# Windowed attention and a squared-ReLU network: where the weights' combinations are made, and how deep their stream runs

## The chip, the cores and the metric

One core of a Trainium2 chip runs the whole program. The metric is the device time of one execution in microseconds (us); a smaller number is better. The engines are named as in the profile: PE (TensorE matmuls), PEld (the loading of PE's stationary operand), DVE (VectorE), ACT (ScalarE), POOL (GpSimd) and SP (SyncE, whose queue issues every DMA of this kernel).

## The reference, cut to what matters

```
# q, k, v: 8 batches x 8 heads x 576 tokens x 64, float32
scores = (q @ k.T) / sqrt(64)
mask   = (0 <= i - j) & (i - j < 64)            # a window of 64 tokens
attn   = softmax(where(mask, scores, -1e9))
x      = (attn @ v), heads side by side         # 4608 tokens x 512
h = x @ w_in                                    # 512 x 2048
r = maximum(h, 0)
out = (r * r) @ w_out                           # 2048 x 512
```

## The kernel before, in words

**Precision.** The large products keep float32 accuracy by splitting each operand into a high part and a rest (`hi`, `lo`, both fp32r), so that each product is three matmuls: hi by hi, hi by lo, lo by hi.

**Tiles and sections.** The 4608 tokens are 12 tiles of 384. The attention is cut into 36 sections, three to a tile. A section's operations have one letter each in `section`: S (scores on PE), o and s (the part of the window that is wanted, copied on ACT and DVE), z and y (negated maximum), e and f (two halves of the exponentials on ACT), k and R (sums and reciprocals), m (the multiplication by the reciprocal, on POOL), X (transposes on PE), x (masked copy on DVE), V (attention by values on PE), H and Q (high part and rest of the result, into the tile that the network reads). Q is only needed for the first four tiles.

**The network.** Tiles 0 to 3 (`NPLAIN = 4`) are done plainly: 16 blocks `f` of the hidden width for each, and for each block 12 matmuls of the first stage (`mm1`, letter M, line 398), then r, p, g, G (ReLU, square, high part and rest: lines 407, 412, 415, 417), then 9 matmuls of the second stage (`mm2`, letter O, line 440), two blocks behind (`LAG = 2`). Tiles 4 to 11 are done in four pairs: the first stage of a pair is a two by two block product with seven products in place of eight (`product`, line 879, 6 matmuls each), in 8 steps for each pair, and the second stage (`second`, line 963) follows two steps behind, three calls of 12 matmuls a step.

**The weights' combinations.** Four of the seven products take a combination of blocks of the first-stage weights rather than a block itself. These are made once, in 16 pieces `h`, by `mix`, and written to a DRAM tensor `mixed`: A (six POOL instructions, lines 526 and 528), C (high part, on ACT, line 530), E (rest, on POOL, line 532), F (the DMA, line 534). A piece works in one half, `h % 2`, of a wide SBUF tile. That tile takes the place of `a_t`, in which the weights are split, so the first A waits for the end of that splitting (operation l15, line 131). The split weights themselves are written to DRAM (`kept`) as well.

**What sets the order.** Up to the second block of tile 2 the order on every engine is written by hand: the string `order`, one token per operation, and each engine does its own operations in the order of the string. From there on `Plan` makes the order: each operation is given an engine, a cost, what it reads and writes, and how long after it its data has landed; `in_order` gives each engine, whenever it comes free in the model, the ready operation with the earliest due time, where due times are counted back from PE's fixed sequence. The order that comes out is fixed before the program runs; on the chip each engine, SP's queue too, works strictly in it.

**What the change touches.** Pieces 0 to 9 (`NMIX = 10`) are in the string, between M22 and M33, together with the sections 6 to 9; pieces 10 to 15 are in the plan, beside tiles 2 and 3. Tiles 4 and 5 are held in the wide tile, tile 4 in half 0 and tile 5 in half 1, so their sections come after the pieces that use the same half. In tiles 2 and 3 a burst of one section (`burst`) is put into PE's sequence at the blocks that `starts` lists: S of section i, V of section i - 1; X of section i comes two blocks later (`crosses`).

In the paired part every product fetches its weight block (256 KB, `wi_fetch`, line 706) into one of 8 slots (`NWI`), each again free when its product is done; every block of the second-stage weights (512 KB, `wo_fetch`, line 714) goes into one of 8 slots (`NWO`). The same SP queue issues the loads of q and k (line 145, eight DMAs a call) and of v (line 154). The seven operands of a pair's products (differences of the tiles' quarters, split into high part and rest) are made by `operands`.

Of the kernel before, what the change touches and what calls it, by code (L numbers as in the profile page):

```python
# [15 lines left out]
P = 128  # L16
# [12 lines left out]
def window_attention_relu2_ffn(ctx: ExitStack, tc: tile.TileContext, q, k, v, w_in, w_out, out):  # L29
# [188 lines left out]
    def section(op, i, eng=None):  # L218
# [81 lines left out]
        else:  # L300
            hi, lo = get_x(i // SPT)
            ps = ps_x[i].rearrange("p m (w q) -> p m w q", q=QB)
            for d, nd, w0, r0, n in regions:
                cols = slice(r0 * QB, (r0 + n) * QB)
                h, l = hi[:, :, d:d + nd, cols], lo[:, :, d:d + nd, cols]
                vals = ps[:, :, w0:w0 + nd * n].rearrange("p m (d r) q -> p m d (r q)", d=nd)
                if nd == 1:
                    h, l, vals = h[:, :, 0], l[:, :, 0], vals[:, :, 0]
                if op == "H":
                    copier(eng or "a")(h, vals)  # L310
                else:
                    dve.tensor_tensor(l, vals, h.bitcast(F32), ALU.subtract)
# [40 lines left out]
    def out_tile(t):  # L353
        if ("out", t) not in xs:
            xs["out", t] = ffn.tile([P, NTB, DM], F32, name="x0" if t else "x1")
        return xs["out", t]
# [117 lines left out]
    while n1 < NF:  # L474
# [24 lines left out]
        g26 F3 Q6 z8 X7 r27 C4 E4 G26 y8 M28 A6 p27a x7 e8 D5 O26 g27 F4 f8 G27 q7 V7 r28 C5 E5 k8 R8 p28a m8p  # L499
        S9 g28 F5 H7d M29 A7 G28 Q7 o9d v10 X8 r29 C6 E6 s9 M30 A8 p29a x8 g29 F6 z9 v11 V8 r30 C7 E7 D6 y9 f9  # L500
        M31 A9 p30d H8a e9 Q8 O27 k9 R9 m9p G29 O28 g30 F7 r31 C8 E8 p31d X9 G30 g31 F8 O29 x9 D7 G31 M32 O30
        r32 C9 E9 p32d g32 F9 M33 G32 O31 r33 Z31 W31 p33d g33 G33"""
# [14 lines left out]
    def mix(op, h):  # L517
        p, kk = divmod(h, 2)
        flat = wide()[:, h % 2].rearrange("p a b c -> p (a b c)")
        scr = flat[:, :4 * P].rearrange("p (a b) -> p a b", a=4)  # L520
        mx = flat[:, 4 * P:12 * P].bitcast(F32R).rearrange("p (a b c) -> p a b c", a=4, b=2)
        if op == "A":
            for c in range(2):
                hi, lo = (wparts[2 * p + c][:, 0, part].bitcast(F32).rearrange("p (a k c) -> p a k c", a=2, k=2)[:, :, kk]
                          for part in range(2))
                pool.tensor_tensor(scr[:, 2 * c:2 * c + 2], hi, lo, ALU.add)  # L526
            for to, a, b, how in ((3, 2, 3, ALU.add), (2, 0, 2, ALU.subtract), (0, 3, 0, ALU.subtract), (1, 1, 0, ALU.subtract)):
                pool.tensor_tensor(scr[:, to], scr[:, a], scr[:, b], how)  # L528
        elif op == "C":
            act.copy(mx[:, :, 0], scr)  # L530
        elif op == "E":
            pool.tensor_tensor(mx[:, :, 1], scr, mx[:, :, 0].bitcast(F32), ALU.subtract)  # L532
        else:
            sp.dma_start(mixed[p, :, :, :, kk * P:(kk + 1) * P], mx.bitcast(F32))
# [77 lines left out]
    def operand(n):  # L612
        if n in (0, 2, 3):
            x = slab(f"xb{max(0, n - 1)}", F32R)[:, :4 * TT].rearrange("p (a b c) -> p a b c", a=2, b=2)
        elif n > 4:
            x = x_tile(3)[:, n - 5]
        else:
            if "x" not in xs:
                xs["x"] = ffn.tile([P, 2, 2, 2, TT], F32R, name="x0")
            x = xs["x"][:, n // 4]  # L620
        return x
# [4 lines left out]
    class Plan:  # L626
# [16 lines left out]
        def in_order(self):  # L643
# [22 lines left out]
            while len(out) < len(ops):  # L666
# [24 lines left out]
    HOP, NEAR = 0.12, 0.05  # L691
# [9 lines left out]
    def wi_fetch(name, source, keys=()):  # L701
# [5 lines left out]
             freed(f"wi{slot // 4}") if n < NWI else [])  # L707

    def wo_fetch(name, f):
        n = wo_n[0]  # L710
        wo_n[0] += 1
        slot = n % NWO
        wo[name] = slot
        plan("sp", 0.1, lambda: sp.dma_start(wo_slot(slot).bitcast(F32), kept[f, :, 1]), [], [("wo", slot)], 6.0,
             freed(f"wo{slot // 2}") if n < NWO else [])
# [6 lines left out]
    def held(i):  # L722
# [3 lines left out]
        return [("XF", half, m, i % SPT) for m in range(2)] + ([("mix", half)] if i // SPT < NPLAIN + 2 else []), []  # L726
# [44 lines left out]
    def settle(i):  # L771
# [3 lines left out]
        plan("act", 0.56, by(section, "H", i), ["v_ps0", "v_ps1"], hi)  # L775
# [3 lines left out]
    def burst(i, late=None):  # L779
        scores(i)  # L780
        values(i - 1 if late is None else late)
        weigh(i)
        settle(i - 1 if late is None else late)
# [3 lines left out]
    def plain1(n):  # L787
# [4 lines left out]
        plan("pe", 1.95, do, [(x, t % 2, r) for x in ("xh", "xl") for r in range(SPT)] + [("w", f)], [("bank", 0)])  # L792
# [33 lines left out]
    def operands(j):  # L826
        keys = {(m, half): [("XF", half, m, r) for r in range(SPT)] for half in range(2) for m in range(2)}
        b = {mh: (lambda m=mh[0], half=mh[1]: wide()[:, half, m], keys[mh]) for mh in keys}
# [8 lines left out]
        def split(n, x):  # L837
            dead = []
            if first and n in (0, 2, 3):
                dead = freed(f"xb{max(0, n - 1)}")  # L840
            elif first:
                dead = [(y, 1, r) for y in ("xh", "xl") for r in range(SPT)] if n > 4 else [("x", tb) for tb in range(NTB)]
# [11 lines left out]
        sub("dve", b[1, 0], b[1, 0], t[1])  # L854
        split(5, b[1, 0])
# [9 lines left out]
    def product(s, n):  # L865
# [16 lines left out]
        plan("pe", 0.98, do, [("xo", n, 0), ("xo", n, 1), ("wi", slot)], [key])  # L882
# [45 lines left out]
    def second(k, x):  # L928
# [49 lines left out]
    starts = {2: 10, 5: 11, 8: 12, 11: 13, 14: 14, 17: 15, 20: 16, 23: 17, 26: 18}  # L978
    crosses = {n + 2: i for n, i in starts.items()}
    for h in range(NMIX, 2 * NP):  # L980
        mixing(h)
    for n in range(2 * NF + LAG, NPLAIN * NF):
        m = n - 2 * NF
        plain1(n)
        if m in starts:
            burst(starts[m])
# [4 lines left out]
        if m % 3 == 0 and 10 <= 9 + m // 3 < NF:  # L991
            plan("sp", 0.1, by(keep, 9 + m // 3), [("w", 9 + m // 3), ("r", n % 2)], [], 8.0)
# [61 lines left out]
```

## Time and profile before

| | us |
|---|---|
| median of 3 runs | 883.92 |
| the runs | 881.0, 883.92, 888.91 |
| the profiled execution | 883.67 |
| its span, first to last instruction | 882.0 |
| PE busy / PEld busy | 842.4 / 770.7 |
| DVE / ACT / POOL busy | 581.9 / 407.7 / 206.0 |
| mean granted TensorE clock | 0.981 |

A row of instructions in the profile gives the line, the engine, the operation, what is written and read, the count, then busy time, the mean in nanoseconds of one, and the idle time ahead of them with what ended it. The chain is the sequence of work that ended last, followed back from the last instruction; its rows give start, duration and what was done, with the count of instructions merged. The matmul rows of the chain are the time by which the chain moved on, a little under the busy time of the same matmuls. The table by windows gives busy time and count of each engine in a stretch, then the granted clock, the share of the DMA engines that was busy and GB/s.

### The profile page before, as it was taken

To read this page: it belongs to the slowest core of one execution; us is meant where nothing else is said; L and a number is where in the kernel's file an instruction comes from. 1 tells how busy PE (TensorE), PEld (TensorE's weight loads), DVE (VectorE), ACT (ScalarE), POOL (GpSimd) and SP (SyncE) were. 2 spreads that over 40 slices of the span, in tenths; PEclk is the share of its full clock that TensorE was granted. 3 is DMA by queue.
4 is the path that set the end of the run, shared out by engine and by line. 5 is a ranking of instruction groups with operands and counts; after the bars stand their busy time and mean duration, and the time that the engine had idled before them with its cause. 6 is when DMAs were issued, how large, how long until landed. Compare 5 with 4: busy or idle time off the path is not lost.

```text
span 882.0 us, 17771 instructions
## 1 busy us (share of the span) xinstructions
PE 842.4 (96%) x6754; PEld 770.7 (87%) x6754; DVE 581.9 (66%) x870; ACT 407.7 (46%) x1127; POOL 206.0 (23%) x258
## 2 busy tenths in 40 slices
PE   6899999779999999999799999999999999999998
PEld 5688998669999998999699998998999999999997
DVE  5799996454575567667368665678765668545553
ACT  5787874554454644554334344434345424222221
POOL 1210008685731112112131111140121141101010
PEclk9899999788999999999899999999999999999999
DMA  9989948575576467849875789968695574767521
GB/s 216 225 265 323 348 168 172 111 161 153 180 180 174 138 124 194 275 123 222 169 231 170 217 237 184 268 200 212 224 280 154 173 232 134 255 232 240 150 104 71
DMA packets 273012, 173.92 MB, mean 197 GB/s; under 512 B 190496, under 2 KB 239648, under 8 KB 270880
## 3 DMA queue, kind: packets, MB, share of 16 engines
q1 hardware_dynamic: 272928, 172.80, 69.9%
q8 instruction: 53, 0.87, 0.4%
q14 instruction: 31, 0.25, 0.1%
HBM read 138.15 MB, written 34.60 MB: 196 GB/s over the span
## 4 chain that ended last, share of the span: by engine, by line
PE 75%; POOL 6%; SPq 5%; DMA 5%; DVE 4%; issue 3%; ACT 2%; POOLq 0%; DVEq 0%; ACTq 0%
PE banks L963 27%; PE banks L879 24%; PE banks L440 9%; PE banks L398 8%; PE banks L232 3%; PE banks L295 3%; POOL a L528 2%; SPq L145 2%; POOL a L526 2%; ACT sel L260 1%; DMA w<-in_moe_w_out_dram 1%; PE banks L273 1%; SPq L182 1%; POOL a L532 1%; DVE a L122 1%
## 5 line engine op out<-in xcount | busy, mean ns | idle before, releaser
L963 PE MATMUL banks<-w 128*128 128x512 f32 x1152 | 258.3, 381 | 0.0
L963 PEld LDWEIGHTS banks<-w 128*128 128x128 f32 x1152 | 216.5, 190 | 28.7
L879 PE MATMUL banks<-x,w 128*128 128x384 f32 x768 | 137.6, 329 | 7.7 <-DMA w<-mixed 4.2
L398 PE MATMUL banks<-x,w 128*128 128x384 f32 x768 | 139.8, 333 | 3.0 <-ACT r L407 2.7
L440 PE MATMUL banks<-w,g 128*128 128x512 f32 x576 | 138.1, 386 | 0.1
L398 PEld LDWEIGHTS banks<-x,w 128*128 128x128 f32 x768 | 129.3, 193 | 7.7 <-ACT r L407 4.9
L879 PEld LDWEIGHTS banks<-x,w 128*128 128x128 f32 x768 | 127.0, 190 | 9.6 <-issue 5.6
L905 POOL TENSOR_TENSOR g<-g 128x384 f32<-128x384 f32 x64 | 57.7, 906 | 320.9 <-ACT g L916 306.8
L440 PEld LDWEIGHTS banks<-w,g 128*128 128x128 f32 x576 | 107.6, 191 | 14.7 <-DVE g L417 1.3
L879 PE MATMUL banks<-w 128*128 128x384 f32 x576 | 107.4, 332 | 0.0
L260 ACT ACTIVATE sel<-sel,nm 128x64 f32<-128x64 f32 x272 | 90.8, 335 | 29.9 <-POOL nm L254 14.9
L879 PEld LDWEIGHTS banks<-w 128*128 128x128 f32 x576 | 96.3, 191 | 2.0
L971 DVE TENSOR_TENSOR w<-w,banks 128x512 f32<-128x512 f32 x72 | 49.4, 686 | 71.2 <-PE banks L963 71.2
L269 POOL TENSOR_TENSOR sel<-sel,nm 128x512 f32<-128x512 f32 x33 | 35.9, 1089 | 145.9 <-DVE nm L266 81.1
L953 ACT CAST w<-w 128x512 fp32r<-128x512 f32 x48 | 29.8, 620 | 73.0 <-PE banks L963 73.0
L953 ACT CAST w<-g 128x512 fp32r<-128x512 f32 x48 | 29.6, 620 | 63.9 <-PE banks L963 61.9
L407 ACT ACTIVATE r<-banks 128x384 f32<-128x384 f32 x64 | 31.6, 493 | 56.8 <-PE banks L398 55.7
L417 DVE TENSOR_TENSOR g<-r,g 128x384 fp32r<-128x384 f32 x64 | 40.8, 639 | 19.5 <-ACT g L415 14.3
L893 DVE TENSOR_TENSOR w<-banks,r 128x384 f32<-128x384 f32 x64 | 38.2, 596 | 20.7 <-PE banks L879 20.5
L260 ACT ACTIVATION_READ_ACCUMULATOR sel<-sel,nm 128x1 f32 x272 | 51.0, 187 | 0.0
L412 DVE TENSOR_TENSOR r<-r 128x384 f32<-128x384 f32 x38 | 25.7, 677 | 35.7 <-ACT r L407 35.7
L277 DVE TENSOR_TENSOR pt<-banks,masks 128x1024 f32<-128x1024 f32 x33 | 40.2, 1218 | 11.7 <-PE banks L273 11.7
(89 smaller groups left out, 1005.0 us busy)
## 6 DMA issues: line engine op xcount, KB each, us to landing
w<-mixed SPq DMA_DIRECT2D x128, 256.0 KB, 4.8
w<-kept SPq DMA_DIRECT2D x64, 512.0 KB, 7.0
w<-kept SPq DMA_DIRECT2D x96, 256.0 KB, 4.9
kept<-w SPq DMA_DIRECT2D x16, 1024.0 KB, 9.0
vt<-in_v_dram SPq DMA_DIRECT2D x144, 64.0 KB, 3.9
w<-in_moe_w_in_dram SPq DMA_DIRECT2D x16, 512.0 KB, 7.4
w<-in_moe_w_out_dram SPq DMA_DIRECT2D x16, 512.0 KB, 8.3
mixed<-a SPq DMA_DIRECT2D x16, 512.0 KB, 3.7
```

The lines of the kernel that those rows point to most:

```text
L260: act.activation(sels[i][:, w, hd], sels[i][:, w, hd], AF.Exp, bias=nms[i][:, n], scale=SCALE, accum_out=sums[i][:, n])
L269: (dve if eng == "d" else pool).tensor_tensor(p, p, rs[i][:, :, None].broadcast_to([P, SW * 2, QB]), ALU.mult)
L277: dve.tensor_tensor(pts[i].rearrange("p (w n) q -> p w n q", n=2), ps_t[i][:, :, None, :].broadcast_to([P, SW, 2, P]), masks.rearrange("p ...
L398: pe.matmul(h_ps, lhsT=weights(kk, part), rhs=in_turn(x[xx][:, kk // 2, kk % 2]), start=n == 0, stop=n == 3 * NK - 1)
L417: dve.tensor_tensor(gs[n][1], rg.pop(n), gs[n][0].bitcast(F32), ALU.subtract)
L440: pe.matmul(acc(t, tb), lhsT=gg[:, ts], rhs=in_turn(weights(part)), start=f == 0 and n == 0, stop=f == NF - 1 and n == 2)
L879: pe.matmul(ps[:, :TT], lhsT=w[:, part, kk * P:(kk + 1) * P], rhs=in_turn(x[:, xx, kk]), start=n < 4 and m == 0, stop=m == 5, skip_group_c ...
L893: plan("dve", 0.6, lambda: dve.tensor_tensor(to(), ps, other(), ALU.add), [kps, ko], keys, 0, after)
L905: plan("pool", 0.95, lambda: pool.tensor_tensor(x(), x(), x(), ALU.mult), [], keys)
L953: plan("act", 0.62, lambda: act.copy(high(c), src()), g_keys, [kh], 0, freed("hi") if new else [])
L963: pe.matmul(ps, lhsT=gg[:, m // 2, m % 2], rhs=in_turn(wo_slot(w[m])[:, part]), start=m == 0 and n == 0, stop=m == 3 and n == 2)
L971: plan("dve", 0.72, lambda: dve.tensor_tensor(by_half(parts(tb)), by_half(parts(tb)), ordered(ps), ALU.add), [key], [kp])
```

## The change

1. `NMIX` goes from 10 to 4: pieces 0 to 3 stay in the hand-written order, now close together between M21 and M25 (A0 C0 E0 A1 C1 E1 and so on, with C right behind its A), and pieces 4 to 15 are in the plan. There A is planned as six single operations, and E goes to DVE instead of POOL; a piece's DMA is planned to land after 5.0 us instead of 8.0.
2. Tile 4 is no longer held in the wide tile but in the second half of the buffer `x0`, whose first half takes tile 2's output; so its sections wait for the end of tile 2's first stage instead of the pieces that use half 0.
3. The sections of tiles 4 and 5 are two deep: after the S of section i comes V of section i - 2, and at the same block, behind the second stage, X of section i - 1. `starts` and `crosses` are rewritten; section 17's V is at block 28 (it was at 26).
4. `NWI` goes from 8 to 13. The five new slots are the unused last quarters of the slabs xb0, xb1, xb2, hi and lo.
5. A fetch of second-stage weights is tied to a product (`tick`): one after each of the products 0, 2, 4 and 6 of every second step, instead of four as soon as their slots are free.
6. The seven operands are laid out otherwise; the first pair's three differences go to DVE instead of POOL.
7. The plan takes 1.5 us instead of 0.12 from an operation of another engine than PE to an SP operation that waits for it.

```diff
-NWI = 8
+NWI = 13
-NMIX = 10
+NMIX = 4
...
     def get_x(t):
...
-        return wide()[:, t % 2], wide()[:, t % 2]
+        if t == NPLAIN:
+            out_tile(2)
+            return xs["out", 2][:, 1], None
+        return wide()[:, t % 2], None
...
         order = """ ...
-        l15 p21a g21 q3 G21 M22 A0 O21 r22 p22d g22 G22 M23 A1 D2 O22 r23 C0 E0 p23d q4 g23 F0 M24 A2 G23 Z22
-        W22 O23 r24 C1 E1 p24d g24 F1 G24 S6 M25 A3 o6a D3 q5 s6 O24 r25 C2 E2 z6 p25a y6 g25 F2 f6 G25 S7 O25
-        e6 o7d s7 v9 k6 z7 M26 A4 R6 y7 m6p f7 D4 X6 e7 q6 S8 x6 r26 C3 E3 k7 V6 R7 o8a p26d m7p M27 A5 H6a s8
+        l15 A0 p21a g21 C0 E0 q3 G21 M22 A1 O21 r22 F0 p22d g22 C1 E1 G22 M23 A2 D2 O22 r23 F1 p23d q4 g23 C2 E2
+        M24 A3 G23 Z22 W22 O23 r24 F2 p24d g24 C3 E3 G24 S6 M25 o6a D3 q5 s6 O24 r25 F3 z6 p25a y6 g25 f6 G25 S7
+        O25 e6 o7d s7 v9 k6 z7 M26 R6 y7 m6p f7 D4 X6 e7 q6 S8 x6 r26 k7 V6 R7 o8a p26d m7p M27 H6a s8 g26 Q6 z8
... (the rest of the string: the same tokens with the pieces 4 to 9 taken out)
+    def wi_home(n):
+        return (f"wi{n // 4}", n % 4) if n < 8 else (("xb0", "xb1", "xb2", "hi", "lo")[n - 8], 3)
...
-                    soon[m] = max(soon[m], start + cost + lands + HOP)
+                    hop = SPARE if ops[m][0] == "sp" and engine != "pe" else HOP
+                    soon[m] = max(soon[m], start + cost + lands + hop)
...
-        plan("pool", 2.9, by(mix, "A", h), w, key)
+        for c in range(6):
+            plan("pool", 0.77 if c < 2 else 0.5, by(mix, "A", h, [c]), w if c < 2 else [], key)
         plan("act", 0.6, by(mix, "C", h), [], key)
-        plan("pool", 1.3, by(mix, "E", h), [], key)
-        plan("sp", 0.1, by(mix, "F", h), key, [("mixed", h // 2, h % 2)], 8.0)
+        plan("dve", 0.7, by(mix, "E", h, dve), [], key)
+        plan("sp", 0.1, by(mix, "F", h), key, [("mixed", h // 2, h % 2)], 5.0)
...
-        sub("pool", t[0], b[0, 1], b[0, 0])
-        sub("pool", t[1], b[1, 1], t[0])
-        sub("pool", b[0, 1], b[1, 1], b[0, 1])
+        eng = "dve" if first else "pool"
+        sub(eng, t[0], b[0, 1], b[0, 0])
+        sub(eng, t[1], b[1, 1], t[0])
+        sub(eng, b[0, 1], b[1, 1], b[0, 1])
...
-        if half == 0 and x == 0:
-            for f in range(4 * group, 4 * group + 4):
-                wo_fetch((j, f), f)
...
-    starts = {2: 10, 5: 11, 8: 12, 11: 13, 14: 14, 17: 15, 20: 16, 23: 17, 26: 18}
-    crosses = {n + 2: i for n, i in starts.items()}
+    starts = {2: (10, 9), 5: (11, 10), 9: (12, 11), 13: (13, 0), 16: (14, 12), 18: (15, 13), 21: (16, 14), 23: (17, 15),
+              26: (18, 16), 28: (0, 17)}
+    crosses = {4: 10, 7: 11, 11: 12, 16: 13, 18: 14, 21: 15, 23: 16, 26: 17, 30: 18}
...
             for n in range(7):
                 product(s, n)
+                if s % 2 == 0 and n % 2 == 0:
+                    f = s % NP * 2 + n // 2
+                    wo_fetch((s // NP, f), f, [("tick", s, n)])
```

A pair in the new `starts` is (section whose S comes here, section whose V comes here); 0 stands for none.

More of the change, by code (lines that the diff above doesn't have):

```diff
@@ L354, in out_tile @@
         if ("out", t) not in xs:
-            xs["out", t] = ffn.tile([P, NTB, DM], F32, name="x0" if t else "x1")
-        return xs["out", t]
+            xs["out", t] = ffn.tile([P, 2, 2, 2, TT], F32, name="x0" if t else "x1")
+        return xs["out", t][:, 0].rearrange("p a b c -> p (a b c)").rearrange("p (n e) -> p n e", n=NTB)
     def slab(name, dtype, words=4 * DM):
@@ L514, in keep, with mix @@
         sp.dma_start(kept[f], wparts[f].bitcast(F32))
-    def mix(op, h):
+    def mix(op, h, which=None):
         p, kk = divmod(h, 2)
@@ L522, in mix @@
         if op == "A":
[L523 to L528, printed above, removed]
+            for c in which or range(6):
+                if c < 2:
+                    hi, lo = (wparts[2 * p + c][:, 0, part].bitcast(F32).rearrange("p (a k c) -> p a k c", a=2, k=2)[:, :, kk]
+                              for part in range(2))
+                    pool.tensor_tensor(scr[:, 2 * c:2 * c + 2], hi, lo, ALU.add)
+                else:
+                    to, a, b, how = ((3, 2, 3, ALU.add), (2, 0, 2, ALU.subtract), (0, 3, 0, ALU.subtract),
+                                     (1, 1, 0, ALU.subtract))[c - 2]
+                    pool.tensor_tensor(scr[:, to], scr[:, a], scr[:, b], how)
         elif op == "C":
@@ L531, in mix @@
         elif op == "E":
-            pool.tensor_tensor(mx[:, :, 1], scr, mx[:, :, 0].bitcast(F32), ALU.subtract)
+            (which or pool).tensor_tensor(mx[:, :, 1], scr, mx[:, :, 0].bitcast(F32), ALU.subtract)
         else:
@@ L612, in operand @@
     def operand(n):
[L613 to L621, printed above, removed]
+        if n < 3:
+            return slab(f"xb{n}", F32R)[:, :4 * TT].rearrange("p (a b c) -> p a b c", a=2, b=2)
+        if n < 5:
+            return x_tile(3)[:, n - 3]
+        if "x" not in xs:
+            xs["x"] = ffn.tile([P, 2, 2, 2, TT], F32R, name="x0")
+        return xs["x"][:, n - 5]
     FULL = (NTILE - NPLAIN) // 2
@@ L689, in in_order @@
             return [ops[n][2] for n in out]
-    HOP, NEAR = 0.12, 0.05
+    HOP, NEAR, SPARE = 0.12, 0.05, 1.5
     plan = Plan()
@@ L706, in wi_fetch, with wo_fetch @@
         plan("sp", 0.1, lambda: sp.dma_start(wi_slot(slot).bitcast(F32), source), keys, [("wi", slot)], 4.5,
-             freed(f"wi{slot // 4}") if n < NWI else [])
-    def wo_fetch(name, f):
+             freed(wi_home(slot)[0]) if n < NWI else [])
+    def wo_fetch(name, f, tick):
         n = wo_n[0]
@@ L713, in wo_fetch @@
         wo[name] = slot
-        plan("sp", 0.1, lambda: sp.dma_start(wo_slot(slot).bitcast(F32), kept[f, :, 1]), [], [("wo", slot)], 6.0,
+        plan("sp", 0.1, lambda: sp.dma_start(wo_slot(slot).bitcast(F32), kept[f, :, 1]), tick, [("wo", slot)], 6.0,
              freed(f"wo{slot // 2}") if n < NWO else [])
@@ L725, in held @@
             return [("xh", i // SPT % 2, i % SPT)], [("xl", i // SPT % 2, i % SPT)]
-        return [("XF", half, m, i % SPT) for m in range(2)] + ([("mix", half)] if i // SPT < NPLAIN + 2 else []), []
+        return [("XF", half, m, i % SPT) for m in range(2)] + ([("mix", half)] if 4 < i // SPT < 7 else []), []
     def scores(i):
@@ L774, in settle, with burst @@
         hi, lo = held(i)
-        plan("act", 0.56, by(section, "H", i), ["v_ps0", "v_ps1"], hi)
+        plan("act", 0.56, by(section, "H", i), ["v_ps0", "v_ps1"], hi, 0,
+             [(x, 0, r) for x in ("xh", "xl") for r in range(SPT)] if i // SPT == NPLAIN else [])
         if lo:
             plan("dve", 0.68, by(section, "Q", i), ["v_ps0", "v_ps1"] + hi, lo)
-    def burst(i, late=None):
+    def burst(i, j):
         scores(i)
-        values(i - 1 if late is None else late)
+        values(j)
         weigh(i)
-        settle(i - 1 if late is None else late)
+        settle(j)
     def plain1(n):
@@ L791, in do @@
             hs[n] = mm1(t, f, lambda kk, part: wparts[f][:, 0, part, kk * P:(kk + 1) * P])
-        plan("pe", 1.95, do, [(x, t % 2, r) for x in ("xh", "xl") for r in range(SPT)] + [("w", f)], [("bank", 0)])
+        plan("pe", 1.95, do, [(x, t % 2, r) for x in ("xh", "xl") for r in range(SPT)] + [("w", f)],
+             [("bank", 0), ("tick", n)])
         plan("act", 0.49, by(evac, "r", n), [("bank", 0)], [("r", n % 2)])
@@ L838, in split @@
             dead = []
-            if first and n in (0, 2, 3):
-                dead = freed(f"xb{max(0, n - 1)}")
+            if first and n < 3:
+                dead = freed(f"xb{n}")
+            elif first and n < 5:
+                dead = [(y, 1, r) for y in ("xh", "xl") for r in range(SPT)]
             elif first:
-                dead = [(y, 1, r) for y in ("xh", "xl") for r in range(SPT)] if n > 4 else [("x", tb) for tb in range(NTB)]
+                dead = [("x", tb) for tb in range(NTB)] + keys[0, 0] + keys[1, 0]
             plan("act", 0.75, lambda: act.copy(operand(n)[:, 0], x[0]()), x[1], [("xo", n, 0)], 0, dead)
@@ L853, in operands @@
         split(4, b[1, 0])
-        sub("dve", b[1, 0], b[1, 0], t[1])
-        split(5, b[1, 0])
+        sub("dve", t[0], b[1, 0], t[1])
+        split(5, t[0])
         split(6, b[1, 1])
@@ L881, in do @@
                     m += 1
-        plan("pe", 0.98, do, [("xo", n, 0), ("xo", n, 1), ("wi", slot)], [key])
+        plan("pe", 0.98, do, [("xo", n, 0), ("xo", n, 1), ("wi", slot)], [key, ("tick", s, n)])
         b, a, c, d = (sums_of.get((s, m), (None, None)) for m in range(4))
@@ L985, in window_attention_relu2_ffn @@
         if m in starts:
-            burst(starts[m])
+            burst(*starts[m])
         plain2(n - LAG)
```

18 lines of the change are left out of this document (9 added, 9 removed).

## The prediction

> **What bounds the kernel now.** First I read the table by windows, for where PE is idle at all: only there can a change that removes no matmul gain time. Columns: stretch, its length, busy time of PE, PEld, DVE, ACT, POOL, granted clock, DMA share, GB/s.
>
> ```profile
> 140.00:160.00 20.00, 16.94 (x142) 14.78 (x140) 10.52 (x14) 9.77 (x30) 15.87 (x25) 0.97 0.83 190
> 160.00:180.00 20.00, 15.93 (x205) 14.36 (x205) 7.83 (x11) 11.65 (x45) 15.51 (x25) 0.77 0.47 99
> 180.00:200.00 20.00, 14.19 (x97) 12.54 (x96) 12.21 (x19) 8.08 (x27) 17.84 (x28) 0.83 0.71 157
> ...
> 220.00:240.00 20.00, 20.00 (x175) 18.62 (x174) 10.97 (x20) 9.19 (x32) 14.53 (x19) 1.00 0.61 196
> ...
> 420.00:440.00 20.00, 13.77 (x126) 12.37 (x125) 8.05 (x16) 6.13 (x24) 2.61 (x3) 0.89 0.83 173
> ```
>
> Two holes lie behind the start-up: 140 to 200, where PE is idle for 12.9 us and the clock is down to 0.77, and 420 to 440, 6.2 us. Nearly everywhere else PE is at 20 of 20. Next the chain, for what fills the first hole.
>
> ```profile
> by line: POOL a L528 23.0%; POOL a L526 17.4%; POOL a L532 13.2%; ACT sel L260 10.4%; PE banks L440 8.9%; issue 7.2%; PE banks L398 5.8%; POOL sel L269 4.4%; ACT r L407 1.6%; DVE w L131 1.5%; PE banks L273 1.4%; ACT a L530 1.3%; POOL nm L26
> ...
> 134.88 1.70 POOL a L526 x2
> ...
> 155.10 0.22 POOL nm L254
> ...
> 155.34 2.77 ACT sel L260 x16
> ...
> 197.34 1.12 PE banks L273 x4
> 198.45 3.84 PE banks L440 x9
> ...
> 204.82 1.29 PE banks L440 x6
> ```
>
> From 134.88 (A0) to 197.34 (X9) the chain runs over POOL: A and E are 54% of 128 to 206. The sections' small POOL operations (y, k, m) wait behind them, PE waits for the sections. O30 starts at 204.82; I use it as the marker. For the second hole, the chain and then SP's queue:
>
> ```profile
> 407.30 7.10 PE banks L879 x42
> ...
> 424.27 3.51 DMA w<-kept
> ...
> 451.62 7.02 PE banks L879 x42
> ```
>
> ```profile
> 406.51 3.13 SPq L714 DMA_DIRECT2D w<-kept  x4
> 409.69 10.05 SPq L154 DMA_DIRECT2D vt<-in_v_dram  x8
> 419.85 0.55 SPq L145 DMA_DIRECT2D raw<-in_q_dram  x1
> ...
> 424.27 0.45 SPq L706 DMA_DIRECT2D w<-kept  x1
> ```
>
> Products start at 407.30, 424.27 and 451.62: one step of 16.97 us, then one of 27.35. From 406.51 to 424.27 SP issues four second-stage fetches, eight loads of v and eight of q and k, and no weight block for a product; with 8 slots for 7 products a step, PE has used what was there by then.
>
> **Part 1: the hand-written order, pieces 0 to 9 become 0 to 3.** The rows with the durations, first PE's (S, V, O, X and M in the chain), then the groups:
>
> ```profile
> 326.05 0.93 PE banks L232 x32
> 326.98 0.89 PE banks L295 x40
> ...
> 336.79 1.94 PE banks L440 x9
> 338.74 0.44 PE banks L273 x4
> 339.17 1.95 PE banks L398 x12
> ```
>
> ```profile
> L528 POOL TENSOR_TENSOR a<-a 128x128 f32<-128x128 f32 x64 | 32.6, 509 | 5.0
> ...
> L526 POOL TENSOR_TENSOR a<-w 128x256 f32<-128x256 f32 x32 | 24.6, 789 | 80.1 <-DVE w L131 79.6
> ...
> L269 POOL TENSOR_TENSOR sel<-sel,nm 128x512 f32<-128x512 f32 x33 | 35.9, 1089 | 145.9 <-DVE nm L266 81.1
> ...
> L532 POOL TENSOR_TENSOR a<-a 128x512 fp32r<-128x512 f32 x16 | 21.6, 1354 | 14.7 <-ACT a L530 14.7
> ...
> L954 DVE TENSOR_TENSOR w<-w 128x512 fp32r<-128x512 f32 x48 | 33.2, 691 | 14.0 <-ACT w L953 14.0
> ...
> L530 ACT CAST a<-a 128x512 fp32r<-128x512 f32 x16 | 9.8, 616 | 2.0 <-POOL a L528 2.0
> ```
>
> With gaps between instructions A is 4.0 us (2 of 789 ns, 4 of 509), C 0.62, E 1.35. The new order puts C right behind its A and E behind that, so POOL stands still during each C: 4.0 + 0.7 + 1.4 = 6.1 us a piece. Walked from A0 at 134.88: A0 ends at 138.9, C0 139.6, E0 141.0; A1 145.0, C1 145.7; A2 151.1, C2 151.8; A3 157.2, C3 157.9, E3 159.2. y6 comes behind E3, at about 160, where it was at 155.10: this part is first **later**, not earlier. ACT is held too: r22 stands behind C0, r23 behind C1, r24 behind C2 and the output copies, o6 behind C3, and each next M needs that r's bank. An M taking 1.95 and an O 1.94, PE waits 1.2 us before M23, 2.2 before M24, 2.9 before M25 and 1.4 before S7. The section chain then runs freely: e and f 2.77 us together, k and R 0.4, m 1.09, so X6 stands at 164.8; before it was at 163.30.
>
> Behind X6 no piece is left. PE's work from X6 to O30 is four X, two S, three V, six M and four O: 1.8 + 1.9 + 2.7 + 11.7 + 7.8 = 25.9 us. I add 1.5, an estimate from the durations, for V6 and V8 behind their x (1.22) and X8 behind Q7: O30 at 192.2. Against 204.82 that gains 12.6. I take **-11**: the walk leaves nothing for engines that meet, and waits of up to 2.9 us cost clock, as these rows show (second column the time):
>
> ```profile
> 182.76 1.02 PE L273 MATMUL banks<-ident,sel 128*128 128x128 f32 x4 [2.57 <-DVE x L312]
> ...
> 183.43 3.58 PE L398 MATMUL banks<-x,w 128*128 128x384 f32 x12
> ```
>
> After 2.57 us of idleness four transposes took 1.02 and an M 3.58 in place of 1.95; before M25 that would be about 2 us, of which ACT and POOL, still behind until 160, hide most. Bounds: if only the two later waits of PE, 2.57 and 3.25 us, go and X6 is 1.5 later, -4; if PE is never kept waiting behind X6, -14. The Trainium skill, "TensorE: Matmul & The Clock Gate" (Part 1), puts the fall to half rate after an idle window of about 3.4 us; by it none of the walk's waits would slow PE and this term would be nearer the walk's -12.6. The row shows the fall after 2.57, so the row decides.
>
> **Part 2: tiles 2 and 3 take six pieces more.** Twelve pieces are 12 x 3.6 = 43 us of POOL (nine m, 10 us, come to that) in some 150 us, 7.4 us of C on ACT, 8.3 us of E on DVE at L954's 691 ns. The row 220:240 has mixing beside bursts of sections, with POOL at 14.53, and PE at 20.00; DVE (10.97) and ACT (9.19) have room. So I cost it at nothing; the cover is PE's own matmuls. The wait that takes the place of another: in the new `starts`, X of one section comes one O (1.94 us) behind V of another, in the same bank, and H must come between. These rows price it:
>
> ```profile
> L310 ACT COPY a<-banks 128x256 f32<-128x256 f32 (+3 forms) x38 | 15.0, 433 | 5.3 <-PE banks L295 4.3 <-DMA raw<-in_k_dram 0.6 <-DVE w L954 0.2
> ...
> 334.57 2.22 PE L398 MATMUL banks<-x,w 128*128 128x384 f32 x12 [0.68 <-ACT r L407]
> ```
>
> H is 0.43 us and half a group of exponentials ahead of it on ACT 1.4 (2.77 / 2), so six joints can each cost 0 to 1. The other end is below nothing: the wait of 0.68 us above, of an M for an r that stood behind exponentials, may go. I take +0.5, range -0.7 to +6.
>
> Queued DVE work is the term's risk. The Trainium skill, "SBUF — State Buffer" (the shared port pair), says that a DVE instruction with two SBUF inputs and a POOL instruction exclude each other for their whole length. It speaks against this change, which puts more POOL work beside DVE's g - hi and E. By it each such pair costs one of them the other's length, up to 0.8 us a time. In the row 220:240 the two are busy for 25.5 of 20 us together, so they do not exclude each other always; no row here shows the lock by itself.
>
> **Part 3: the hand-over to the pairs.** Section 17's V is the row at 326.98 above; the products began here, and the rows under it price the operands:
>
> ```profile
> 354.74 6.83 PE banks L879 x42
> ```
>
> ```profile
> L844 DVE TENSOR_TENSOR x<-a,x 128x768 fp32r<-128x768 f32 x16 | 15.2, 947 | 0.2 <-ACT x L843 0.2
> ...
> L834 DVE TENSOR_TENSOR a<-a,w 128x768 f32<-128x768 f32 x4 | 5.4, 1350 | 0.0
> ```
>
> 26.9 us of cover lay between; V moves two blocks of 3.9 us, so 19 us (a stall of 0.7 taken off 26.9) less 1 remain, about 18. What must fit: H 0.8, two differences of 1.35, one more, a split of 0.95 on DVE: the first operand by 7 us, all seven by about 19, where the sixth and seventh product need theirs at 18 + 5. DVE also has to do p, G and section 18's steps, some 8 us. It fits with little left: +0.5, range 0 to 5 (each of the four differences taking twice its time).
>
> **Part 4: 13 slots, second-stage fetches spread.** SP's hole of 17.8 us lies beside a step of 17.0. With 13 slots the fetches issued ahead reach 12 products ahead at the start of the hole: the next step's first six blocks are there at 424.27, and its seventh is issued first behind the hole, 6 us before its product. What is late next: nothing that PE reads, since SP catches up in the following step (7 fetches of 0.45 us, 3.2 in all). Gain 27.35 - 17.05 = 10.3, clock loss within it. A smaller stall of the same kind:
>
> ```profile
> 515.13 7.02 PE banks L879 x42
> ...
> 534.38 4.94 DMA w<-mixed
> ...
> 550.58 7.02 PE banks L879 x42
> ```
>
> Its two steps took 35.45 against 34.1: 1.3. Together **-11**, taking both as gone but 0.6; bounds 0 (SP's total of issues is the same, and the jam only moves) and -11.6. The ticks put fetches a step behind their present place, yet the second stage reads them two steps, 34 us, later: nothing.
>
> **The sum.** 883.67 (the profiled execution; median of the runs 883.92) - 11 + 0.5 + 0.5 - 11 = **862.7 us**. 1% of the time is 8.8 us, about what this measurement can tell from no change.
>
> **The rivals.**
> Both holes shrink: 862.7, own range 856 to 869. Chance 0.60.
> *The first hole only moves.* The four pieces hold ACT and POOL until 159, and the sections behind them take as long as before: part 1 gives -2, the rest holds: 871.7. For it: y6 is 5 us later by my walk. Against: 54% of that chain is A and E, and six of ten are gone. 0.14.
> *The second hole only moves.* SP's issues are the limit in the first pair and the 13 slots only put the stall into a later step: 873.7. For it: 17.8 us without a pause in SP's rows. Against: five slots more cover 5 products, and behind 451.62 the longest such stall is the one of 1.3 us. 0.12.
> *Tiles 2 and 3 lose what is gained*, by the joints and operands at their upper ends (+6 and +5) and part 4 half: 883.7 - 11 + 6 + 5 - 5.5 = 878. 0.08.
> *The pieces stall PE in tiles 2 and 3.* C waits in ACT's queue for an A that POOL, kept off by DVE, ends late; r stands behind C, and the next M behind r, as in my walk of M23 to M25: 2.1 us of wait and about 2 of slow clock for each of twelve pieces, +49; with the rest kept, 912. It decides once POOL falls behind its plan by more than a block (3.9 us). Against: no such wait from 204 to 320 with six pieces there. This is also what the rule of the port pair would make of the time. 0.06.
>
> **How the numbers follow.** Under 875: the first case, nearly all of the second, and most of the third: 0.82. Within 1%: the fourth and the rest, 0.12. Slower: 0.06. Range 856 to 876: it holds the first three cases; what is left out is the last two and a little.
>
> **What would show it.** In the changed profile: O30 some 11 us earlier than 204.82, y6 later than 155.10, POOL no more in the chain behind 165; waits of PE for ACT's r before M23 to M25; PE at 20 of 20 from 200 to 340 with E on DVE at 0.7; no wait of products for `mixed` or `kept`, and every step with a section at 17.1. I am wrong if PE waits for ACT in tiles 2 and 3, if the first product of the pairs waits for its operands, or if SP's queue is again ahead of PE with loads while slots stand empty.

## The result, and the profile after

The changed kernel took **861.70 us** (median of 4 runs, 861.0 to 863.32) beside 883.67 (881.0 to 888.91) for the kernel before on the same chip: ratio 0.9747, 95% interval 0.97 to 0.9794. The forecast was 862.7, with a range of 856 to 876. The profiled execution took 862.08, its span is 860.3 (before 883.67 and 882.0), so the spans differ by 21.7.

Two matters of reading first. The lines of the helpers have moved: M is now L401, O is L443, the products are L894, the second stage L975; A is L529 and L533, C L535, E L537. And five marks cut the span into parts that can be set beside each other: the end of l15 (the last instruction ahead of A0), X6, O30, the first product of the pairs, and the end.

The table by windows, the same stretches as before:

```profile
140.00:160.00 20.00, 15.37 (x125) 12.13 (x124) 10.72 (x13) 7.04 (x14) 16.80 (x24) 1.00 0.75 176
160.00:180.00 20.00, 16.48 (x215) 14.72 (x215) 11.70 (x20) 12.97 (x58) 8.63 (x18) 0.91 0.48 91
180.00:200.00 20.00, 19.86 (x144) 18.16 (x143) 11.95 (x18) 8.54 (x28) 1.52 (x3) 1.00 0.68 146
220.00:240.00 20.00, 20.00 (x172) 18.61 (x171) 13.31 (x24) 10.05 (x33) 10.02 (x15) 1.00 0.53 175
420.00:440.00 20.00, 20.00 (x173) 18.51 (x172) 14.59 (x23) 8.27 (x27) 8.99 (x7) 1.00 0.92 206
```

The hole at 420 is gone. Of the first one 8.2 us of idleness are left between 140 and 180 (4.63 and 3.52); from 180 to 200 PE is at 19.86 of 20, where before it had 14.19. The chain from 128 to 206, by line and then in order of time:

```profile
by line: PE banks L401 24.3%; PE banks L443 19.1%; POOL a L533 14.7%; POOL a L529 12.7%; POOL a L537 6.5%; PE banks L295 5.9%; PE banks L232 4.2%; ACT a L535 3.2%; issue 2.6%; ACT r L410 1.9%; DVE w L131 1.5%; PE banks L273 1.4%; POOL sel L
...
133.15 1.70 POOL a L529 x2
...
157.29 3.13 POOL a L529 x4
160.42 0.20 POOL nm L254
160.63 3.32 POOL a L533 x8
...
165.75 0.66 PE banks L273 x4
...
195.04 1.94 PE banks L443 x9
```

A and E are 34% of it, not 54, and behind X6 (165.75) POOL is off the chain. O30 starts at 195.04 in place of 204.82. But between E3, which ends at 157.22, and y6 (L254) stand four instructions of A that the string has nowhere near.

The chain in the pairs, where each first product of a step begins:

```profile
344.10 3.39 PE banks L894 x21
347.50 6.03 DMA w<-kept
...
353.54 8.96 DMA vt<-in_v_dram
...
363.77 7.02 PE banks L894 x42
...
380.92 7.02 PE banks L894 x42
...
397.99 7.02 PE banks L894 x42
...
414.94 7.02 PE banks L894 x42
...
431.99 7.02 PE banks L894 x42
```

17.15, 17.07, 16.95 and 17.05 us a step; the last of them, from 414.94, is the one that took 27.35 before (from 424.27). Part by part, with the experiments told of below (all in us; each column is the length of the stretch up to the mark):

| kernel | end of l15 | to X6 | to O30 | to the first product | to the end |
|---|---|---|---|---|---|
| before | 134.81 | 28.5 | 41.5 | 149.92 | 527.26 |
| after | 133.08 | 32.7 | 29.3 | 149.06 | 516.20 |
| after_8slots | 133.02 | 32.6 | 29.3 | 149.07 | 526.32 |
| before_13slots | 133.31 | 28.3 | 41.3 | 149.70 | 514.56 |
| after_one_block | 135.58 | 30.1 | 28.2 | 149.06 | 516.93 |
| old_places | 131.56 | 24.9 | 29.3 | 149.07 | 515.90 |
| after_0pieces | 133.98 | 22.0 | 28.1 | 169.66 | 516.57 |
| odd_pieces_early | 133.05 | 22.0 | 28.1 | 149.07 | 515.89 |
| odd_no_ticks | 133.42 | 22.0 | 28.1 | 149.06 | 514.63 |
| after_no_ticks | 133.34 | 32.6 | 29.6 | 149.07 | 514.82 |
| after_E_on_pool | 130.85 | 32.6 | 29.2 | 149.06 | 516.61 |

The 21.7 us of after against before are 1.7 in the start, 8.0 from l15 to O30 (70.01 to 61.96), 0.9 in tiles 2 and 3, and 11.1 in the pairs. The first of them is no gain of the change: up to l15 the hand-written order is the same in all eleven kernels, and l15 ends anywhere from 130.85 to 135.58.

### The profile page after: what moved, and what is told of

Its sections match the earlier page's. It is cut to its first block, busy times and chain, and to the rows that moved or that the text cites. A ratio compares the mean times of both kernels' runs of the same rounds, so it can differ in the third digit from the quotient of the medians.

```text
span 860.3 us, 17706 instructions
## 1 busy us (share of the span) xinstructions
PE 832.6 (97%) x6754; PEld 762.0 (89%) x6754; DVE 591.1 (69%) x885; ACT 409.0 (48%) x1127; POOL 186.4 (22%) x243
## 4 chain that ended last, share of the span: by engine, by line
PE 81%; DMA 5%; POOL 4%; SPq 3%; DVE 3%; issue 2%; ACT 1%; DVEq 0%; POOLq 0%; ACTq 0%
PE banks L975 29%; PE banks L894 25%; PE banks L443 9%; PE banks L401 9%; PE banks L295 3%; PE banks L232 3%; DMA w<-in_moe_w_out_dram 3%; PE banks L273 1%; POOL a L533 1%; SPq L182 1%; POOL a L529 1%; DMA vt<-in_v_dram 1%; DVE a L122 1%; SPq L154 1%; DMA w<-kept 1%
## 5 line engine op out<-in xcount | busy, mean ns | idle before, releaser
L975 PE MATMUL banks<-w 128*128 128x512 f32 x1152 | 257.5, 380 | 0.0
L975 PEld LDWEIGHTS banks<-w 128*128 128x128 f32 x1152 | 215.7, 189 | 28.4
L401 PE MATMUL banks<-x,w 128*128 128x384 f32 x768 | 137.6, 329 | 4.0 <-ACT r L410 3.5
L443 PE MATMUL banks<-w,g 128*128 128x512 f32 x576 | 136.6, 382 | 1.0 <-DVE g L420 0.8
L401 PEld LDWEIGHTS banks<-x,w 128*128 128x128 f32 x768 | 126.7, 189 | 9.0 <-ACT r L410 6.4
L894 PE MATMUL banks<-x,w 128*128 128x384 f32 x768 | 130.0, 326 | 0.0
L894 PEld LDWEIGHTS banks<-x,w 128*128 128x128 f32 x768 | 125.7, 189 | 0.0
L443 PEld LDWEIGHTS banks<-w,g 128*128 128x128 f32 x576 | 106.0, 189 | 16.0 <-DVE g L420 2.8
L894 PE MATMUL banks<-w 128*128 128x384 f32 x576 | 100.7, 329 | 0.0
L894 PEld LDWEIGHTS banks<-w 128*128 128x128 f32 x576 | 93.8, 189 | 2.0
L965 ACT CAST w<-g 128x512 fp32r<-128x512 f32 x48 | 29.6, 621 | 62.1 <-PE banks L975 60.1
L420 DVE TENSOR_TENSOR g<-r,g 128x384 fp32r<-128x384 f32 x64 | 38.7, 605 | 19.4 <-ACT g L418 10.1
L913 DVE SCALAR_TENSOR_TENSOR w<-w 128x384 f32<-128x384 f32 x64 | 45.7, 714 | 1.7
```

What stands on the lines that cost most here:

```text
L401: pe.matmul(h_ps, lhsT=weights(kk, part), rhs=in_turn(x[xx][:, kk // 2, kk % 2]), start=n == 0, stop=n == 3 * NK - 1)
L420: dve.tensor_tensor(gs[n][1], rg.pop(n), gs[n][0].bitcast(F32), ALU.subtract)
L443: pe.matmul(acc(t, tb), lhsT=gg[:, ts], rhs=in_turn(weights(part)), start=f == 0 and n == 0, stop=f == NF - 1 and n == 2)
L894: pe.matmul(ps[:, :TT], lhsT=w[:, part, kk * P:(kk + 1) * P], rhs=in_turn(x[:, xx, kk]), start=n < 4 and m == 0, stop=m == 5, skip_group_c ...
L913: plan("dve", 0.57, lambda: dve.scalar_tensor_tensor(x(), x(), 0.0, x(), ALU.max, ALU.mult), [], keys)
L965: plan("act", 0.62, lambda: act.copy(high(c), src()), g_keys, [kh], 0, freed("hi") if new else [])
```

## The experiments

The theory after the result: part 4's gain is the slots' alone; part 1 lost 3 us against the walk because POOL's order is not the string's; tiles 2 and 3 hide the pieces. The rivals: the ticks or the two-deep sections clear SP's queue; the four early pieces cost what the walk left out (engines that meet, slow clock); and twelve pieces beside tiles 2 and 3 hang on E being on DVE.

### The slots alone, from both sides

```diff
# after_8slots: the kernel after
-NWI = 13
+NWI = 8
# before_13slots: the kernel before
-NWI = 8
+NWI = 13
+    def wi_home(n):
+        return (f"wi{n // 4}", n % 4) if n < 8 else (("xb0", "xb1", "xb2", "hi", "lo")[n - 8], 3)
```

> The changed kernel with 8 slots for the first-stage weights instead of 13; all else as changed, the spread fetches of second-stage weights too. If the slots end the stall at the fifth step of the pairs: the stall of about 10 us is back, 871.5 to 873 us, with a wait of products for mixed or kept near 415 us. If spreading the second-stage fetches or the later places of SP's operations in the plan did it: 861 to 863 us.

> The kernel before with 13 slots (the five new ones in the same slabs) and nothing else of the change. If the slots alone are enough: 872 to 873.5 us, steps of the pairs at 17.1 us, no wait for mixed or kept. If SP's issues are the limit and the stall only moves: 880 to 884 us with a stall at a later step.

Measured: after_8slots 871.23 us, ratio 0.9859 [0.982, 0.9898]; before_13slots 868.53, ratio 0.9837 [0.9805, 0.9869]. The pairs take 526.3 and 514.6 us: with the slots alone 12.7 less than before, with all but the slots 0.9 less. The first lies 0.3 under the range expected for a returned stall. The second lies 3.5 under the 872 us expected of the slots alone; l15 ended 1.5 earlier there than in before, and the slots were worth more than the 10.3 and 1.3 of the two stalls that the prediction saw. Beside the rest of the change, from after_8slots to after, the same slots gave 10.1 and not 12.7: 0.9 is what the rest wins with eight slots, and with thirteen the rest loses 1.6, of which the ticks below are 1.4. The chain of after_8slots, and under it that of before_13slots, from the first product on:

```profile
351.34 8.36 DMA w<-mixed
...
416.20 7.59 DMA w<-mixed
...
532.68 4.59 DMA w<-mixed
...
586.98 5.59 DMA w<-mixed
```

```profile
352.54 6.83 PE banks L883 x42
...
361.06 7.04 PE banks L883 x42
...
370.88 7.02 PE banks L883 x42
```

With eight slots products wait for weight blocks again, four times on the chain; spread fetches and two-deep sections don't cure it. With thirteen, in before_13slots, PE waits for no weight block. Where the 12.7 come from is seen by laying the steps of before and of after side by side: 27.35 against 17.05, and two smaller ones, 532.18 to 550.58 against 512.54 to 529.48 (18.40 and 16.94) and, for two steps, 584.78 to 615.48 against 563.68 to 593.51 (30.70 and 29.83): 10.3 + 1.5 + 0.9. These rows of before's chain show the last two stalls, the second of which the prediction didn't see:

```profile
532.18 1.19 PE banks L879 x6
...
539.45 1.21 PE banks L879 x6
...
584.78 1.19 PE banks L879 x6
...
604.49 3.22 PE banks L879 x18
...
615.48 6.83 PE banks L879 x42
```

### The ticks

```diff
# after_no_ticks: the kernel after, second-stage weights fetched as in the kernel before
+        if half == 0 and x == 0:
+            for f in range(4 * group, 4 * group + 4):
+                wo_fetch((j, f), f, [])
...
-                if s % 2 == 0 and n % 2 == 0:
-                    f = s % NP * 2 + n // 2
-                    wo_fetch((s // NP, f), f, [("tick", s, n)])
```

> The changed kernel with the second-stage fetches planned as before the change, four as soon as slots are free, not tied to products. With 13 slots alone on the kernel before, the paired part took 514.6 us, in the changed kernel 516.2. If the ticks cost that, by putting fetches among the first weight blocks and the loads of v: 514.6 to 515.2 us here, 1 us less in all. If they are worth something beside the slots: a stall comes back, 518 us or more. If neither: 516 us.

Measured: 861.61 us, ratio 0.9748 [0.9711, 0.9786]. The pairs take 514.8 in place of 516.2, so the ticks cost 1.4. Two steps took 19.67 us in after (344.10 to 363.77); here, and in before_13slots (352.54 to 370.88), they take 18.35 and 18.34:

```profile
344.58 6.83 PE banks L894 x42
...
362.93 7.02 PE banks L894 x42
```

In after a V waits for `vt` there (the row 353.54 above). SP issued that load 9.4 us behind the first product, four ticked fetches standing among the weight blocks ahead of it in the queue, and only when one of those weight blocks had landed (the row 347.50); the load then took 8.96 us to land. Without the ticks it went out 7.3 us behind (351.86), and none of the loads of v there took more than 5.5. The total doesn't show the 1.4 (861.61 and 861.70): from l15 to O30 this execution took 0.2 longer and its l15 was 0.3 later, and single runs scatter by more. In the pair odd_pieces_early and odd_no_ticks below it is seen again: 515.9 and 514.6 us, and 851.32 and 849.59 in the medians, whose intervals overlap.

### POOL's order: one scheduled block

The program hands its instructions to the scheduler in two blocks, the string and the plan. Written as one, the twelve POOL instructions of the plan's pieces 4 and 5 go back behind the string's, and with three output DMAs nothing else changes place.

```diff
# after_one_block: the kernel after
     with tc.manual_schedule(engines={E.PE, E.DVE, E.Activation, E.Pool, E.SP}):
         for token in order.split():
...
-    with tc.manual_schedule(engines={E.PE, E.DVE, E.Activation, E.Pool, E.SP}):
-        for do in plan.in_order():
-            do()
+        for do in plan.in_order():
+            do()
```

> The changed kernel with the hand-written order and the plan in one scheduled block, so that the twelve POOL instructions of pieces 4 and 5 stand behind section 9's m instead of around section 6's y; the order of DVE and ACT is the same, three output DMAs on SP move by a few places. If these twelve instructions (6.5 us on POOL) are what made the transposes of section 6 wait: the transposes come about 2.5 us earlier against the first A, the slow matmuls behind them are gone (2 us), 856.5 to 859 us. If ACT and PE's own order set that place: 861 to 863 us.

Measured: 860.02 us, ratio 0.9742 [0.9707, 0.9777]. Its chain:

```profile
160.42 0.62 POOL nm L254
...
165.64 0.67 PE banks L273 x4
...
193.81 1.94 PE banks L443 x9
```

l15 ended at 135.58 here, so y6 stands 24.8 behind it where after has it 27.3 behind, X6 30.1 (the walk: 30.0) and O30 58.2 (the walk: 57.4; after: 62.0). Of the 3.7 us, 2.6 are A's four instructions ahead of y6 and 1.1 the slower clock behind X6. The eight further ones (the row 160.63 of after, 3.32) cost little: they ran while ACT did e6. The total fell by only 1.7, whose interval overlaps after's, and 860.02 lies between the two ranges expected (856.5 to 859 and 861 to 863). In the profiled execution l15 ended 2.5 later than in after; the stretch behind it, from l15 to O30, is what settles the question.

### No early piece at all

```diff
# after_0pieces: the kernel after; A, C, E, F of pieces 0 to 3 taken out of the string
-NMIX = 4
+NMIX = 0
```

> The changed kernel with all 16 pieces in the plan and none in the hand-written order. If the four pieces there are what is left of the first hole: no C holds ACT, O30 comes 49 to 52 us behind the end of the weights' splitting instead of 62, and the total is 849 to 853 us. If sixteen pieces are too many beside tiles 2 and 3: PE waits there for ACT or for tile 5's half, 858 us or more.

Measured: 869.93 us, ratio 0.9851 [0.9814, 0.9889]. The stretch from l15 to O30 came down to 50.1, with X6 never late. What was won was given back in tiles 2 and 3: 169.7 us in place of 149.1. The waits from 280 to 330, then the window 300 to 320, then SP's row of the last F:

```profile
PE banks L273 <- ACT a L310: 17.5, 1, 17.5
...
ACT a L310 <- DMA mixed<-a: 10.4, 1, 10.4
```

```profile
300.00:320.00 20.00, 8.99 (x36) 8.61 (x37) 3.57 (x5) 2.11 (x4) 4.69 (x7) 0.58 0.61 108
```

```profile
306.44 1.24 SPq L520 DMA_DIRECT2D mixed<-a  x2
```

With all sixteen pieces in the plan the last ones that use half 1 of the wide tile come late; the last two F stand on SP behind 16 loads of q and k (issued from 294.09 on), and H of section 15, which writes tile 5 into that half, waits for it on ACT. PE waits 17.5 us behind, and its granted clock falls to 0.58. So the early pieces are there for a reason: two of those in half 1 are enough, as the next kernel shows.

### Two early pieces, where nothing waits for them

```diff
# odd_pieces_early: the kernel after in one block; pieces 1 and 3 in the string, 14 in the plan
-l15 A0 p21a g21 C0 E0 q3 G21 M22 A1 O21 r22 F0 p22d g22 C1 E1 G22 M23 A2 D2 O22 r23 F1 p23d q4 g23 C2 E2 M24 A3 ...
+l15 A1 p21a g21 q3 G21 M22 O21 r22 p22d g22 C1 E1 G22 M23 D2 O22 r23 F1 A3 p23d q4 g23 M24 ... r24 C3 E3 p24d g24 F3 ...
-    for h in range(NMIX, 2 * NP):
+    for h in [h for h in range(2 * NP) if h not in (1, 3)]:
# odd_no_ticks: the same, and the second-stage fetches as in after_no_ticks
```

> One block, and only the pieces 1 and 3 in the hand-written order, their C placed behind an r that is due anyway, so that neither ACT nor y6 waits for them; the other fourteen in the plan, so that the half of the wide tile which tile 5 needs has six planned pieces as in the changed kernel and the other half eight. If the four early pieces are what is left of the first hole, and the half of tile 5 is what the kernel without early pieces ran into: O30 49 to 52 us behind the end of the splitting (62 in the changed kernel), tiles 2 and 3 at 149 us as there, total 849 to 853 us. If fourteen planned pieces are too many whatever half they use: a wait of PE near 290 us, 858 us or more.

> Both of the above in one: pieces 1 and 3 early, one block, second-stage fetches as before the change. If the two do not touch each other: 1 to 1.5 us less than with the pieces alone, 848 to 852 us. If the ticks matter more when POOL and SP are later: as with the pieces alone or slower.

Measured: 851.32 us, ratio 0.9636 [0.959, 0.9681], and without ticks **849.59**, ratio 0.9609 [0.9575, 0.9644], the best of these kernels. The windows of odd_pieces_early have PE at 19.7 of 20 where after had 15.37 and 16.48:

```profile
140.00:160.00 20.00, 19.72 (x220) 17.46 (x219) 13.23 (x20) 12.98 (x47) 7.56 (x13) 1.00 0.82 176
160.00:180.00 20.00, 19.71 (x214) 17.57 (x213) 13.92 (x23) 12.15 (x46) 6.14 (x10) 1.00 0.40 71
```

50.1 us from l15 to O30 is what the same stretch takes with no piece at all. The fourteen pieces beside tiles 2 and 3 cost nothing: 149.07.

### Is it the number of early pieces, or their place?

```diff
# old_places: the kernel after in one block, pieces 0 to 3 where the string had them before
-l15 A0 p21a g21 C0 E0 q3 G21 M22 A1 O21 r22 F0 p22d g22 C1 E1 G22 M23 A2 D2 O22 r23 F1 p23d q4 g23 C2 E2 M24 A3 ...
+l15 p21a g21 q3 G21 M22 A0 O21 r22 p22d g22 G22 M23 A1 D2 O22 r23 C0 E0 p23d q4 g23 F0 M24 A2 ... r24 C1 E1 ...
+... M25 A3 o6a D3 q5 s6 O24 r25 C2 E2 z6 p25a y6 ... x6 r26 C3 E3 ...
```

> The kernel after in one scheduled block, with the early pieces 0 to 3 written at the places that they had in the string before (A0 after M22, C and E of a piece steps behind its A, with the first-stage operations between them on ScalarE and VectorE), where the string of after_one_block has C right behind A and E ahead of y6. Still four early pieces and no more. Measured so far from the end of step 15's first-stage work to step 30's second-stage product: 69.5 to 70.0 us with pieces 0 to 9 early in the old places, 58.2 with 0 to 3 early in the new ones (after_one_block), 50.1 with none or two that ride behind operations that are due anyway. Theory (what a piece costs there is set by where it stands: the product waits only when C holds ScalarE's queue ahead of operations that PE is waiting for): the stretch takes 53 to 54.5 us, and the time is 855 to 858 us. Rival (the number of early pieces sets it, some 2 us each, wherever they stand): 57 to 58.5 us, and 859 to 862 us. From the product on, tiles 2 and 3 take 149 us and the rest 516 to 517 us by both.

Measured: 853.66 us, ratio 0.9682 [0.964, 0.9725]. From l15 to O30 it took 54.2 us, in the theory's 53 to 54.5 and 4.1 under the new places (58.2); the time is 1.3 below the theory's lower end, and l15 ended early in the profiled execution (131.56). The chain (E is L518 in this kernel) and, from PE's rows, X6 with what follows:

```profile
150.39 1.24 POOL a L518
151.63 0.21 POOL nm L254
...
185.73 1.94 PE banks L443 x9
```

```profile
156.42 0.66 PE L273 MATMUL banks<-ident,sel 128*128 128x128 f32 x4 [2.71 <-POOL sel L269]
157.01 1.98 PE L232 MATMUL banks<-qk 64*64 64x128 f32 x32
158.75 1.91 PE L295 MATMUL banks<-pt,vt 64*64 64x128 f32 x40
```

y6 stands 20.1 behind l15, not 24.8: POOL no longer stands still while C is made (four times 0.7), and E3 (1.3) is behind y6. PE doesn't wait for an r, where after_one_block has 2.1 us of it and 2.5 more ahead of S6 and S7 (for the output copies on ACT and for s on DVE). What remains against 50.1 is one wait of 2.71 and the slow matmuls behind it. So the place of four pieces is worth 4.1 us, and a fixed price of some 2 us a piece wherever it stands is refuted. The number counts as well, and for more: from ten pieces (before) to four in the old places the stretch fell by 15.8 us (70.0 to 54.2).

### E on POOL in the plan

```diff
# after_E_on_pool: the kernel after
-        plan("dve", 0.7, by(mix, "E", h, dve), [], key)
+        plan("pool", 1.3, by(mix, "E", h), [], key)
```

> The changed kernel with E of the twelve planned pieces on POOL, at the cost of 1.3 us that the plan gave it before. In the changed kernel the DMA of piece 15 is issued at 296.8 us and the first part of tile 5 is written to the same half at about 302. If that is a near thing: six pieces longer by 0.65 us each make PE wait at V of section 15 or 16, and tiles 2 and 3 take 151 to 153 us from O30 to the first product instead of 149.1. If there is room, or moving E off DVE gives POOL and DVE back what they cost each other: 148.8 to 149.3 us.

Measured: 861.23 us (2 runs), ratio 0.974 [0.9684, 0.9796]; tiles 2 and 3 take 149.06 as with E on DVE, so what I had put down as a near thing (151 to 153) did not come. Its windows:

```profile
220.00:240.00 20.00, 20.00 (x171) 18.51 (x170) 12.59 (x18) 10.09 (x34) 14.22 (x19) 1.00 0.51 153
...
260.00:280.00 20.00, 20.00 (x243) 18.43 (x242) 12.48 (x21) 13.97 (x50) 14.95 (x21) 1.00 0.95 259
```

POOL has 14 to 15 of 20 where after has 10.02 in the first of these, and PE is at 20.00 by either.

Not tried by themselves: the two-deep sections, which can't be taken away alone because tile 4 has moved into `x0`, the operands' layout, and the plan's other new costs (A as six operations, 5.0 us for a piece's DMA, 1.5 us ahead of SP).

## Why the prediction was right, and where it wasn't

The total hit by 1 us, with terms that were further off: part 1 fell short by 3.0, and parts 2 and 3 (1.9 better) and the start (1.7) made that good. So the total is closer than the terms are, and that much of it is luck.

**Part 1, said -11, measured -8.0.** The step that failed is the walk's premise that POOL does its operations in the order of the string. The walk itself was right where that holds: E3's end 24.3 us behind A0's start (measured 24.1), and in after_one_block X6 30.1 behind l15 (walked 30.0) and O30 58.2 (57.4). In the program that ran, the first two instructions each of A4 and A5, 3.13 us, came between E3 and y6. PE's rows of after show the waits that were forecast, 1.2, 2.2, 2.9 and 1.4 before M23, M24, M25 and S7 (the four rows ahead of X6 are M23, M24, S6, behind which M25 stands, and S7):

```profile
138.08 2.22 PE L401 MATMUL banks<-x,w 128*128 128x384 f32 x12 [0.90 <-ACT r L410]
...
144.11 2.22 PE L401 MATMUL banks<-x,w 128*128 128x384 f32 x12 [1.19 <-ACT r L410]
...
150.24 1.58 PE L232 MATMUL banks<-qk 64*64 64x128 f32 x32 [1.28 <-ACT x L452]
...
157.18 1.10 PE L232 MATMUL banks<-qk 64*64 64x128 f32 x32 [1.27 <-DVE sel L250]
...
165.75 0.66 PE L273 MATMUL banks<-ident,sel 128*128 128x128 f32 x4 [3.38 <-POOL sel L269]
166.33 1.61 PE L232 MATMUL banks<-qk 64*64 64x128 f32 x32
167.72 1.98 PE L295 MATMUL banks<-pt,vt 64*64 64x128 f32 x40
169.63 2.48 PE L401 MATMUL banks<-x,w 128*128 128x384 f32 x12
```

They are there and shorter, none as long as 2.9; an O behind M23 and one behind M24 waited 0.42 more for g. The clock was lost not there (it was granted in full from 140 to 160) but behind X6's wait of 3.38: from 166.8 to 170.2 it was granted at 0.50, and S8, V6 and M27 took 1.61, 1.98 and 2.48 where the same stretch of odd_pieces_early has 1.10 and 1.12 for S and V, and M elsewhere 2.22. From X6 to O30 after took 29.3 us, after_one_block, whose wait was 0.78, 28.2. The bound of -4 to -14 held. One reading of the walk was off: it set the 3.58 us of a slow M, a busy time, against the chain's 1.95, where the busy time of an M is 2.22 (the row 138.08), so that M lost 1.4 us and not 1.6. The Trainium skill, "TensorE: Matmul & The Clock Gate" (Part 1), puts the fall at an idle window of about 3.4 us; the wait of 3.38 fits that, but old_places slowed its S to 1.98 after 2.71 us (granted clock 0.50 from 157.1 to 160.5), and in after_8slots the clock fell to 0.50 behind a wait of 1.91 (592.9 to 596.1); there the measurement decides against it.

**Part 2, said +0.5, and part 3, +0.5: measured -0.9 together.** The step that failed is the joints' price: V, H and X one O apart cost nothing, nor did the operands; the wait of 0.68 for r, which I had put at the lower end, is gone. From O30 to the first product PE has no wait in after, and seven more kernels agree to 0.01 us. E on DVE was dearer than its row (815 ns on average, not L954's 691) without consequence for PE. The mean hides two sorts: ten of the twelve ran while POOL did nothing and took 0.65 to 0.70 us, and the two that began while an m ran on POOL (at 211.42 and 225.55) took 1.49. That agrees with the rule of the port pair, which the prediction takes from the Trainium skill, "SBUF — State Buffer" (the shared port pair), and with the prediction's price of up to 0.8 us a time. The stall of PE that the prediction's last rival drew from it didn't come: PE was at 20.00 of 20 there, and moving E from one engine to the other changed nothing for it. One sum of part 3 was off too: 26.9 less 0.7, 7.8 and 1 leaves a cover of 17.4 us, not about 18; it was enough.

**Part 4, said -11, measured -11.1, for other reasons.** The slots gave -12.7, beyond the bound of -11.6: there was a third stall, at 600, of 0.9, and the 0.6 that I kept back was gone too. The step "ticks: nothing" failed: I looked at when the second stage reads its weights, and not at what stands behind them in SP's queue; +1.4. The 0.2 that is left has no cause that was tried.

**The start** gave 1.7 that no step had, by scatter.

Of the rivals, "the first hole only moves" had its half right: y6 was 5.3 us later than before (7.1 counted from the end of l15). What it left out is that nothing stands behind X6. "The pieces stall PE in tiles 2 and 3" came true in one kernel, after_0pieces, by another road than C in ACT's queue: a half of the wide tile that came free late.

## What to carry to other kernels

Work put beside a full engine is dear by where it stands as well as by how much it is: four pieces cost 8.1 or 4.1 us by their places, six more in the old places cost 15.8, and two that were placed behind work that was due anyway cost 0. Whether four could be placed so wasn't tried. Read the order that the program has on each engine, not the one that was written, before walking it. And where an in-order queue issues loads for several consumers, slots that allow a longer lead pay for its bursts; ordering the fetches more evenly didn't here, and held up what stood behind them.

## What was not expected of the hardware

- The end of l15, with the same order ahead of it, came between 130.85 and 135.58 us in eleven executions. A difference of 2 us between two kernels here has to be read from marks behind it. It goes in part with the granted clock of the stretch from 28 to 42 us: 1.00 in the earliest (after_E_on_pool), 0.76 in the latest (after_one_block), in before and in after_no_ticks, 0.88 in the other seven. It isn't the whole of it (in after_no_ticks l15 ended at 133.34), and what makes the clock fall there in some executions stays open.
- Tiles 2 and 3 took 149.06 or 149.07 us in eight kernels with twelve or fourteen pieces beside them: a full PE shows nothing of what the other engines do.
- Not every slow group of matmuls is the clock. S6 took 1.58 us after a wait of 1.28, S7 1.10 after 1.27, in after and in after_one_block alike; but the granted clock was 1.00 there (150 to 152 in after). S6's weight load, which stood still for the output copies on ACT, stood still for them a second time, 0.29 us, after its first four loads.
- Where the clock fell in these two kernels, it stayed at 0.50 for 3.4 us: from 166.8 to 170.2 in after, from 157.1 to 160.5 in old_places. Such a fall cost the stretch from X6 to O30 1.1 to 1.2 us (29.3 in place of 28.1 or 28.2).
- An instruction of DVE can be held up by one of POOL: the two E on DVE that began while POOL's m ran took 1.49 us, the ten others 0.65 to 0.70.
